# A convolution and SiLU block on one core: a new order of the steady block's steps

## The chip, the cores and the metric

The kernel runs on one core of one Trainium2 chip. The metric is the device time of one execution in microseconds (us). Three runs are shown for the kernel before, and the median counts. Engine names are those of the profile: PE multiplies, PEld loads weights for it, DVE is the vector engine, ACT the scalar engine, POOL is GpSimd, and SP issues transfers.

## The reference

The input x has 8 sequences of 4096 tokens with 192 channels, all float32. A causal depthwise convolution with 7 taps comes first; its taps are a softmax over 7 weights for each of 8 heads (24 channels each). Its result, 32768 tokens by 192, goes through a two-layer block without a bias:

```
out[s] = sum over k of softmax(weight)[head, k] * x_padded[s + k]     # 7 taps
h = out @ w_in        # 192 -> 2048
g = h * sigmoid(h)    # silu
y = g @ w_out         # 2048 -> 192
```

## The kernel before

**Blocks and stages.** The tokens are worked in 32 blocks of 1024 (TT = 1024, two halves of 512 columns). The products use fewer multiplications than the plain formula: sums of inputs and of weights are formed so that 15 products stand for 18 in each of five groups of the first layer. For PE a block has two stages. In the first (the P stage below) 75 products and a plain rest make h; in the second (the D stage) 192 matmuls in 48 slots make y. The two alternate for the whole kernel: the P stage of block b, then the D stage of block b.

**Two lanes.** A product of the P stage has 64 rows of weights and 512 columns, and it takes either the upper or the lower half of PE's rows. I call these halves lane 0 and lane 1; `e` in `product` (L616 to L637) picks the lane, and `ON_B` (L599) lists the products of lane 1. Products of the two lanes run at the same time. Each product is two rows of the trace, since a float32 matmul is two passes. In a D slot four matmuls of 128 x 32 weights run side by side in the four column groups.

**The order is written out by hand.** Every engine works its own instructions in the order of issue, and that order is a string of steps. `START` serves the first blocks, and `PLAN` is run once for each later block, from b = 3 on (end of the function). A step is a name and digits, and a sign in front says which block it belongs to: none is block b, `-` is b - 1, `=` is b - 2, `+` is b + 1. The function `step` (L863) calls the helper. The steps are these:

| step | engine | what it does | line of the profile |
|---|---|---|---|
| `Pr.g` | PE | product r of group g, in a chain's PSUM bank | L630 |
| `L.nk` | PE | plain products of the rest; `L.1k` is two halves, one on each lane | L647 |
| `uo.g` | ACT | copy of the running sum of chain 0 to an SBUF tile u | L679 |
| `Xo.g`, `ao.g`, `bo.g` | DVE | add or subtract u, chain 1 (X, a) and chain 2 (b) | L673 |
| `So.g`, `SL.i` | ACT | silu into the tile g | L691, L696 |
| `t.ji` | DVE | differences of g tiles for the second layer | L714 |
| `Di.je` | PE | slot i of the second layer for tile j, half e | L746 |
| `x`, `y`, `z` / `M` | ACT / DVE | copies and sums that finish y | L804 to L824 |
| `o.i`, `st.i` | DVE, SP | transpose of y and three stores | L834, L843 |
| `ld.k`, `i.k` | SP, DVE | four loads of x for the block after next in `+` form, and their transpose | L181, L465 |
| `ha.0` | POOL, SP | the 6 columns of the convolution's past | L486, L487 |
| `v.ki` | ACT, POOL | tap i of channels k of the next block: ACT multiplies into a tile u, and POOL issues a transfer that adds it to nat (tap 0 is ACT alone) | L496, L499, L500 |
| `sp.k`, `w.i` | SP, DVE | copies of nat into dup, and the differences win, which are the products' inputs | L521, L538, L541 |

**What ties the steps together.** In a group, chain 0 is the products 5, 2, 6, 1, 0, 14 in one bank, and after each of the first five a `u` copies the sum before the next product may write. Chain 1 is 3, 9, 7, 4, 8 in a second bank: `X2` reads it after 3, `X4` after 9, `a5` after 7, `a1` after 4, `a0` after 8. Chain 2 is 12, 10 in bank 4, read by `b1` and `b5`. `S3` reads chain 0's bank at its end, and the next group in that bank may start only then. The groups run in the order 0, 4, 1, 2, 3. The slots D0 to D5 write banks 7, 1, 3, 5, 6 and 4, which the P stage uses too, so the last readers of one stage hold the first writers of the other (`P5.4` writes bank 1, and waits for `M2`, the last reader of D1's sum). The tile u comes from a list of ten (`free`): `u` and `v` take from its front, and a tile goes back to its end at once after `v` and after its `X` or `a`. So a `u` can be handed a tile that a POOL transfer is still reading, and then ACT waits for that transfer:

```python
            z = free.pop(0)
            pin(nc.scalar.activation(z, src, AF.Copy, scale=tap))
            pin(nc.gpsimd.dma_start(out=dst, in_=z, accum_op=ALU.add))
            free.append(z)
```

The taps of one k all add to the same nat, so the transfers of `v.k1` to `v.k6` follow one another. The tiles t and osb share three buffers, so `t.10` waits until the stores of the y before it have left.

Of the kernel before, what the change touches and what calls it, by code (L numbers as in the profile page):

```python
# [17 lines left out]
def kernel(  # L18
# [60 lines left out]


    PLAN = (
        "+ld.1 P5.0 | -P8.3 -S1.4 -a0.2 -S4.3 | -D0.00 -t.01 -S0.2 | -D1.00 -S1.2 =o.2 v.00 "
        "| -D2.01 -t.03 -S5.1 =st.2 | -D2.00 -b5.3 | -D1.20 -sp.0 v.21 -S5.3 | -D4.01 u5.0 "
        "-t.02 -S1.3 | -D5.01 -sp.2 | -D4.00 -t.10 | -D0.20 -t.11 | -D3.01 | -D0.11 -t.12 | "
        "-D1.30 v.22 | -D3.00 +ld.2 -t.13 | -D2.11 -a0.3 | -D5.00 | -D2.10 -t.20 -S0.3 | "
        "-D3.11 v.11 | -D5.10 | -D4.11 -w.0 | -D0.30 v.12 | -D4.10 -t.21 | -D1.11 -t.23 | "
        "-D0.21 | -D0.01 v.23 -w.1 | -D3.10 -t.22 | -D5.21 | -D0.31 | -D5.11 | -D1.10 -t.30 "
        "| -D1.01 -t.31 | -D2.20 | -D2.21 v.13 | -D5.20 | -D4.21 v.01 v.14 | -D4.20 v.24 | "
        "-D1.21 -w.2 | -D3.20 -t.33 | -D2.30 v.02 | -D1.31 -t.32 | -D2.31 -y1.0 | -D5.30 "
        "v.03 | -D0.10 v.25 | -D3.21 -z1.0 v.15 -y0.0 | -D4.31 -y2.0 -w.3 | -D5.31 -M1.0 | "  # L90
        "-D3.30 -x2.1 v.26 -x2.0 | -D4.30 -x2.2 -M2.0 | -D3.31 -w.5 -x0.0 -M3.0 | L.02 | "
        "P2.0 -x2.3 -w.4 | P5.4 | P3.0 u4.0 -M6.0 | L.12 v.16 u5.4 | L.00 | P6.0 -x1.0 -M4.0 "
        "| L.10 u2.0 | P2.4 | L.01 X2.0 | L.11 v.04 u4.4 | P9.0 | P1.0 SL.0 -M5.0 SL.2 | "
        "P6.4 | P13.0 u0.0 X4.0 SL.1 | P5.1 | P3.4 -M7.0 S2.0 +i.2 u2.4 | P0.0 | P7.0 X2.4 | "
        "P11.0 | P12.0 u1.0 a5.0 -o.1 | P9.4 | P1.4 S4.0 b1.0 -st.1 u5.1 | P13.4 | P4.0 X4.4 "
        "u0.4 | P10.0 | P2.1 a1.0 +ld.0 v.05 | P7.4 | P0.4 u4.1 b5.0 | P14.0 | P8.0 u1.4 "
        "v.06 S5.0 | P11.4 | P14.4 a5.4 S3.0 a0.0 S2.4 | P6.1 | P12.4 S3.4 | P4.4 | P3.1 "
        "u2.1 b1.4 S4.4 | P5.2 | P10.4 X2.1 | P1.1 a1.4 u5.2 | P9.1 b5.4 | P2.2 u0.1 | P8.4 "
        "X4.1 | P5.3 u4.2 | P7.1 a0.4 | P0.1 +i.1 u5.3 sp.1 | P12.1 a5.1 | P6.2 u1.1 | P3.2 "
        "-o.0 | P4.1 u2.2 b1.1 | P13.1 | P2.3 a1.1 | P10.1 S2.1 | P1.2 u4.3 X2.2 | P8.1 | "  # L100
        "P11.1 -o.3 u0.2 | P13.2 S1.1 a0.1 | P6.3 S4.1 | P9.2 +i.0 | P0.2 b5.1 u2.3 +ha.0 | "
        "P3.3 S0.0 X4.2 | P1.3 S2.2 | P12.2 u1.2 | P11.2 X2.3 | P7.2 u0.3 b1.2 | P14.1 S4.2 "
        "| P9.3 a5.2 S0.4 | P0.3 -st.0 | P10.2 S1.0 X4.3 | P14.2 u1.3 | P7.3 b5.2 +v.20 "
        "-st.3 | P4.2 S0.1 | P12.3 a5.3 S3.1 | P14.3 +v.10 a1.2 | P13.3 | P4.3 S5.2 b1.3 | "
        "P8.2 S2.3 | P11.3 a1.3 S3.3 | P10.3 S5.4 t.00 S3.2"
    )
    START = (
        "=dp.28 =v.20 =v.10 =dp.44 =v.00 =dp.18 =dp.6 =dp.40 =dp.7 =dp.32 =dp.23 =dp.30 "
        "=dp.13 =dp.2 =dp.20 =dp.24 =dp.15 =dp.35 =dp.14 =dp.33 =dp.11 -ld.1 =dp.37 =dp.36 "
        "=dp.25 -ld.2 =dp.27 =dp.17 -ld.0 =dp.0 =v.11 =dp.34 =v.01 =dp.26 =v.12 =dp.29 =v.21 "  # L110
        "=v.13 =dp.45 =v.22 =dp.21 =v.02 =dp.42 =v.14 =v.03 =dp.39 =v.15 =dp.3 =v.04 =dp.38 "
        "=v.16 =dp.47 =v.23 =sp.1 =v.05 =dp.1 =v.24 =dp.22 -i.1 =dp.12 =v.25 =v.06 =dp.43 "
        "=v.26 =go.2 =sp.0 =dp.19 -i.0 =dp.46 -i.2 =dp.31 -ha.0 =dp.9 =sp.2 =dp.4 =dp.41 "
        "-v.10 -v.00 -v.11 =dp.8 -v.20 -v.01 =dp.5 -v.12 =dp.16 -v.02 =w.0 =dp.10 =w.1 =cp.0 "
        "-L.01 -P5.0 -v.03 =cp.1 -L.02 -P5.4 =w.2 -u5.0 -L.10 =w.3 -u5.4 -P2.0 -P3.0 -v.13 "
        "-P2.4 -u4.0 -v.04 -P6.0 -L.00 -u4.4 -L.12 -u2.0 -L.11 -SL.0 -X2.0 -P6.4 -SL.2 =w.4 "
        "=cp.2 -P9.0 -P1.0 -u2.4 =o.0 -P13.0 -P5.1 -v.14 -u0.0 -X4.0 -P3.4 -P1.4 -S2.0 =w.5 "
        "-SL.1 -P7.0 -P11.0 -u5.1 -X2.4 -u0.4 -P12.0 -P0.0 -a5.0 -v.21 -P13.4 -P0.4 -u1.0 "
        "=o.1 -P4.0 -P9.4 -u1.4 -v.15 -S4.0 -P2.1 -P14.4 -a1.0 -b1.0 -P14.0 -P8.0 -u4.1 -X4.4 "
        "-S3.4 -P6.1 -P10.0 -v.22 -S2.4 -a0.0 -P11.4 -P7.4 -u2.1 -b5.0 -S3.0 -P5.2 -P3.1 "  # L120
        "-S4.4 -a5.4 -P1.1 -P12.4 -u5.2 -X2.1 -P4.4 -u0.1 -P9.1 -b1.4 -P2.2 -a1.4 -P10.4 "
        "-X4.1 -P5.3 -u4.2 -P8.4 =o.2 -P6.2 -b5.4 -P13.1 -u5.3 =st.2 -a0.4 -P0.1 -P7.1 -u2.2 "
        "-v.23 -S2.1 ld.1 -P2.3 -P3.2 -a5.1 -u1.1 -S0.0 -P1.2 -P12.1 -X2.2 -S0.4 -P4.1 -u4.3 "
        "-P13.2 -b1.1 ld.2 -S1.4 -P6.3 -a1.1 -u0.2 -P10.1 -v.24 -P11.1 -u2.3 -P8.1 -b5.1 "
        "-P0.2 -S4.1 -P9.2 -v.05 -S2.2 -a0.1 -P12.2 -P1.3 -u1.2 -X4.2 -S0.1 -P3.3 -P14.1 "
        "-b1.2 -u0.3 -S5.4 -P7.2 -P11.2 -X2.3 -v.16 -P10.2 -P0.3 -S4.2 -a5.2 -sp.1 -P9.3 "
        "-P14.2 -u1.3 -b5.2 -S3.1 -P13.3 -P4.2 -X4.3 -S3.2 -S1.0 i.1 -P14.3 -P12.3 =st.0 "
        "-S1.1 -a1.2 -P11.3 -P7.3 -S5.0 -v.06 -S1.2 -t.00 -D0.00 =st.1 -S3.3 -S2.3 -D1.20 "
        "-b1.3 -S5.1 ld.0 -S4.3 -t.01 -D0.01 -S5.2 -D0.21 -t.02 -D1.11 -sp.0 -a5.3 -D1.10 "
        "-v.25 -t.03 -P8.2 P5.0 +ld.1 -P4.3 -P10.3 -D1.30 -b5.3 -v.26 -D1.00 -a0.2 -sp.2 "  # L130
        "-D4.01 -t.10 -S0.2 -D5.00 -D2.01 i.0 -D4.00 -t.11 -D2.00 i.2 -D5.01 ha.0 -t.13 "
        "-D0.11 -D3.00 -a1.3 +ld.2 -D3.01 -t.12 v.10 -D4.11 -w.0 v.00 +ld.0 -D5.10 v.11 v.20 "
        "-D5.11 -D2.10 u5.0 -t.20 -D0.20 -w.1 -D3.11 -t.21 -D4.10 -w.2 -D2.11 -t.23 -P8.3 "
        "P2.0 -D0.31 -a0.3 -t.22 -D3.10 -S0.3 -S1.3 -D4.21 v.21 -S5.3 u4.0 v.01 -D4.20 -t.30 "
        "-D3.20 -D5.21 -t.31 -D2.20 -D5.20 -D2.21 -D0.10 -t.32 -D2.30 v.02 -D1.01 -t.33 "
        "-D0.30 v.03 -D1.31 v.12 -D2.31 v.04 v.22 -D1.21 v.05 -D3.30 -y1.0 -w.3 -z1.0 -D5.30 "
        "v.13 -D5.31 -D3.31 -x2.0 -M1.0 -x2.1 -D4.31 -x2.2 v.14 -x2.3 -y2.0 -M2.0 -D3.21 "
        "-y0.0 v.06 -D4.30 -x0.0 -w.4 v.23 -x1.0 P3.0 P5.4 -M3.0 L.10 u5.4 -w.5 P6.0 L.02 "
        "-M4.0 L.11 u2.0 L.00 P2.4 X2.0 P1.0 L.01 -M5.0 u4.4 v.15 L.12 u0.0 P6.4 P9.0 SL.2 "
        "SL.0 P0.0 P13.0 X4.0 SL.1 u2.4 -M7.0 P3.4 P5.1 S2.0 +i.0 P7.0 P1.4 u5.1 X2.4 P12.0 "  # L140
        "P11.0 u0.4 a5.0 u1.0 v.24 P9.4 P2.1 S4.0 b1.0 P4.0 P13.4 u4.1 X4.4 P14.0 P10.0 a1.0 "
        "P0.4 P7.4 S3.0 b5.0 v.25 P11.4 P8.0 u1.4 a5.4 S2.4 P6.1 P12.4 a0.0 P14.4 P4.4 u2.1 "
        "b1.4 v.26 P5.3 P3.1 S3.4 a1.4 S4.4 P10.4 P1.1 X2.1 P5.2 P8.4 -M6.0 u0.1 b5.4 P9.1 "
        "P0.1 u5.2 -o.1 u5.3 P13.1 P2.2 X4.1 -st.1 u1.1 +i.2 P12.1 P2.3 u4.2 a0.4 S2.1 P7.1 "
        "P6.2 b1.1 u4.3 P3.2 a5.1 P6.3 u2.2 P10.1 S5.4 X2.2 P4.1 u2.3 S0.4 P9.2 b5.1 P1.2 "
        "S0.0 a1.1 P13.2 P11.1 S1.0 -o.0 u0.2 P8.1 v.16 P1.3 S2.2 S4.1 sp.1 P0.2 P12.2 a0.1 "
        "u0.3 X4.2 S5.0 P3.3 P14.1 u1.2 +i.1 P7.2 P11.2 X2.3 -st.0 b1.2 P9.3 P0.3 S4.2 a5.2 "
        "+ha.0 P10.2 u1.3 X4.3 P4.2 S0.1 P7.3 b5.2 P14.3 S1.1 a1.2 S3.1 P12.3 P14.2 S3.3 a5.3 "
        "P13.3 -o.3 P4.3 S3.2 b1.3 -st.3 +v.10 P8.2 +v.20 a1.3 P10.3 P11.3 S5.2 t.00 S2.3"
    )  # L150
    QUEUE = (0, 4, 1, 2, 3)
    CHAIN_BANKS = ((0, 1, 7, 1, 0), (2, 3, 2, 3, 2), (4, 4, 4, 4, 4))
# [41 lines left out]
    x0 = x.flatten_outer_dims()[TB - pad : TB, :].rearrange("t (k c) -> c k t", k=NK)  # L194
# [651 lines left out]
                )  # L846
            )

    plan = [slot.split() for slot in PLAN.split("|")]
    did, later = set(), []  # L850
    closing = f"S3.{QUEUE[-1]}"
    BACK = {"-": 1, "=": 2, "+": -1}
# [263 lines left out]
```

## Time and profile before

| what | value |
|---|---|
| median of three runs | 2364.05 us (2362.52 to 2364.63) |
| span of the profiled execution, first to last instruction | 2358.8 us |
| median less this span | 5.25 us |
| PE busy | 2350.1 us (100%), x17630 |
| PEld busy | 1053.1 us (45%) |
| DVE busy | 1784.5 us (76%) |
| ACT busy | 1488.6 us (63%) |
| POOL busy | 531.0 us (23%) |
| mean granted TensorE clock | 0.999 |
| one P stage, 974.30 to 1010.46 us | 36.16 us |
| the D stage after it, 1010.46 to 1046.67 us | 36.21 us |

The profile is of one execution. It gives that execution's span, and not its whole time; the runs' median stands 5.25 us above the span. PE counts as busy while any matmul is under way, so a lane that stands still beside a working one does not show in the busy share. To see that, one has to read the starts of the single rows: two passes in one lane are 0.429 us apart when nothing holds them.

### The profile page before, as it was taken

What the parts mean: (1) busy time and instruction counts of PE and PEld (TensorE: products, weight loads), DVE (VectorE), ACT (ScalarE), POOL (GpSimd) and SP (SyncE); (2) the same over time, 40 slices, a digit from 0 to 9 for tenths busy, and PEclk for the clock granted to TensorE, in tenths of its full rate; (3) what the DMA queues carried; (4) which work ended last, traced back from release to release, by engine and by line L of the source; (5) the groups of instructions that cost most, each with busy time, mean ns of one, the idle gap of its engine ahead of it and who ended that gap; (6) DMA issues with size and microseconds to landing.
All of it is one profiled execution on the core that took longest, in us unless ns stands there. A gap on an engine that the chain in (4) does not pass through costs nothing.

```text
span 2358.8 us, 45531 instructions
## 1 busy us (share of the span) xinstructions
PE 2350.1 (100%) x17630; PEld 1053.1 (45%) x17630; DVE 1784.5 (76%) x2373; ACT 1488.6 (63%) x2779; POOL 531.0 (23%) x672
## 2 busy tenths in 40 slices
PE   9999999999999999999999999999999999999998
PEld 4344444444444444444444454444444444444445
DVE  8898767787777787777877777767778777787676
ACT  5346766667656677566676666765667756667643
POOL 4911122211222112222112221122211222211200
PEclk9999999999999999999999999999999999999999
DMA  7234667656566655666556656556655566565511
GB/s 158 51 66 72 107 106 125 105 103 107 98 121 107 106 105 95 119 116 106 106 106 109 119 99 109 105 99 122 107 106 101 101 116 116 106 109 98 96 23 25
DMA packets 523833, 238.81 MB, mean 101 GB/s; under 512 B 431648, under 2 KB 436768, under 8 KB 523616
## 3 DMA queue, kind: packets, MB, share of 16 engines
q0 software_dynamic: 73024, 133.73, 33.7%
q1 hardware_dynamic: 447392, 101.78, 23.1%
q8 instruction: 138, 2.26, 0.4%
q10 hardware_dynamic: 3200, 0.39, 0.1%
q14 instruction: 79, 0.65, 0.1%
HBM read 31.46 MB, written 25.17 MB: 24 GB/s over the span
## 4 chain that ended last, share of the span: by engine, by line
PE 98%; DVE 1%; DMA 0%; ACT 0%; SPq 0%; issue 0%; ACTq 0%
PE ps L746 47%; PE ps L630 42%; PE ps L647 5%; PE ps L767 2%; PE ps L576 2%; PE ps L1015 1%; DVE t L714 0%; DMA dup<-nat 0%; PE ps L423 0%; ACT g L691 0%; DMA nat<-u 0%; SPq L843 0%; DVE g L673 0%; DVE cmb L163 0%; ACT u L163 0%
## 5 line engine op out<-in xcount | busy, mean ns | idle before, releaser
L500 POOL DMA_DIRECT2D nat<-u x504 | 431.9, 957 | 1598.0 <-ACT u L499 643.4
L630 PE MATMUL ps<-win,wr 64*128 64x512 f32 x1550 | 721.5, 598 | 0.0
L746 PE MATMUL ps<-g,wo 128*32 128x512 f32 x2976 | 703.0, 593 | 0.0
L630 PE MATMUL ps<-win,ws 64*128 64x512 f32 x1550 | 638.3, 599 | 0.9 <-ACT u L679 0.9
L746 PE MATMUL ps<-t,wo 128*32 128x512 f32 (+2 forms) x4528 | 547.8, 446 | 0.0
L679 ACT COPY u<-ps 128x512 f32<-128x512 f32 x775 | 442.5, 587 | 136.7 <-PE ps L630 88.6
L746 PE MATMUL ps<-t,wx 128*32 128x512 f32 x2976 | 495.6, 592 | 0.6 <-DVE t L714 0.5
L630 PE MATMUL ps<-dup,wr 64*128 64x512 f32 x868 | 424.1, 597 | 0.0
L691 ACT ACTIVATE g<-g 128x512 f32<-128x512 f32 x465 | 286.2, 633 | 175.5 <-DVE g L673 175.5
L714 DVE TENSOR_TENSOR t<-g,t 128x1024 f32<-128x1024 f32 x248 | 302.0, 1218 | 109.7 <-PE ps L746 107.4
L714 DVE TENSOR_TENSOR t<-g 128x1024 f32<-128x1024 f32 x248 | 302.5, 1220 | 103.9 <-PE ps L746 82.7
L809 ACT COPY yx<-ps 32x512 f32<-32x512 f32 x150 | 86.8, 579 | 421.5 <-PE ps L746 419.4
L673 DVE TENSOR_TENSOR g<-u,ps 128x512 f32<-128x512 f32 x465 | 314.2, 681 | 42.8 <-PE ps L630 32.0
L499 ACT ACTIVATE u<-xt,taps 128x512 f32<-128x512 f32 x504 | 340.0, 717 | 1.1
L630 PEld LDWEIGHTS ps<-win,wr 64*128 64x128 f32 x1550 | 272.1, 186 | 139.5 <-issue 75.6
L630 PE MATMUL ps<-dup,ws 64*128 64x512 f32 x682 | 328.2, 598 | 0.0
L630 PEld LDWEIGHTS ps<-win,ws 64*128 64x128 f32 x1550 | 255.8, 186 | 135.3 <-issue 58.6
L746 PEld LDWEIGHTS ps<-t,wo 128*32 128x32 f32 x4528 | 188.5, 110 | 273.3 <-issue 266.0
L691 ACT ACTIVATE g<-ps 128x512 f32<-128x512 f32 x465 | 267.8, 599 | 36.2 <-PE ps L630 33.6
L673 DVE TENSOR_TENSOR ps<-u,ps 128x512 f32<-128x512 f32 x310 | 215.0, 694 | 64.3 <-PE ps L630 26.7
L746 PE MATMUL ps<-g,wx 128*32 128x512 f32 x1488 | 250.5, 592 | 0.0
L824 DVE TENSOR_TENSOR cmb<-cmb,ps 96x512 f32<-96x512 f32 x150 | 102.2, 681 | 181.7 <-ACT yx L809 180.7
(92 smaller groups left out, 2010.5 us busy)
## 6 DMA issues: line engine op xcount, KB each, us to landing
nat<-u POOLq DMA_DIRECT2D x504, 256.0 KB, 4.0
dup<-nat SPq DMA_DIRECT2D x345, 128.0 KB, 3.0
nat<-in_x_dram SPq DMA_DIRECT2D x382, 64.0 KB, 2.7
out_dram<-osb SPq DMA_DIRECT2D x376, 64.0 KB, 2.0
raw<-in_moe_w_out_dram SPq DMA_DIRECT2D x8, 384.0 KB, 3.5
raw<-in_moe_w_in_dram SPq DMA_DIRECT2D x12, 192.0 KB, 4.4
ws<-wr POOLq DMA_DIRECT2D x8, 192.0 KB, 5.0
raw<-in_moe_w_in_dram SPq DMA_DIRECT2D x6, 128.0 KB, 3.0
```

What stands on the lines that cost most here:

```text
L499: pin(nc.scalar.activation(z, src, AF.Copy, scale=tap))
L500: pin(nc.gpsimd.dma_start(out=dst, in_=z, accum_op=ALU.add))
L576: nc.tensor.matmul(hs[a, n, e], rows(wr[j], e)[:, a, k, :], rows(d, e)[:, n, k, :], start=k == 0, stop=k == NK - 1,)
L630: nc.tensor.matmul(to[:, cols], raw(g, *LEFT[e][r], e), rhs[:, cols], start=first, stop=True, skip_group_check=True,)
L647: nc.tensor.matmul(banks[PLAIN_BANKS[n and 1 + e]][:, cols], rows(wr[j] if own == e else ws[j], e)[:, a, k, :], rows(dups[b], e)[:, SLOT[e ...
L673: pin(nc.vector.tensor_tensor(out_, u, v, op=op))
L679: pin(nc.scalar.copy(us[b, g, o][:, cols], t1[:, cols]))
L691: pin(nc.scalar.activation(h, src, AF.Silu))
L714: pin(nc.vector.tensor_tensor(t[i // 2][:, i % 2, :], u, v, op=ALU.subtract))
L746: nc.tensor.matmul(accs[b][at][SQ * q : SQ * q + SQ, to], lhs[:, e, SQ * k : SQ * k + SQ], rhs[:, e, ts(q, TB // 4) if i == 5 else to], st ...
L809: pin(nc.scalar.copy(to, acc[3 * (name[0] == "x") + k][n:P, :]))
L824: pin(nc.vector.tensor_tensor(out_, u, v, op=ALU.add))
```

## The change

`PLAN` gets another order. The bars between slots go, and with them nothing else, since the loop ran through all slots in a row before as well. The multiset of a cycle's steps is the same, but some steps at the seam of two cycles are now counted in the neighbouring one: `=o.2 =st.2` become `-o.2 -st.2`, `-S1.4` becomes `S1.4`, `v.21` becomes `+v.21`, `+v.10` becomes `v.10`, and `S0.1`, `S1.1`, `S2.3`, `S5.4`, `a1.3`, `P10.3` and `t.00` move behind the seam with a `-`. `START` keeps its order and gets four steps at its end, so that the seam fits (its other lines in the diff are only broken anew). No step's operation, tile or bank changes.

```diff
     PLAN = (
-        "+ld.1 P5.0 | -P8.3 -S1.4 -a0.2 -S4.3 | -D0.00 -t.01 -S0.2 | -D1.00 -S1.2 =o.2 v.00 "
-        "| -D2.01 -t.03 -S5.1 =st.2 | -D2.00 -b5.3 | -D1.20 -sp.0 v.21 -S5.3 | -D4.01 u5.0 "
-        "-t.02 -S1.3 | -D5.01 -sp.2 | -D4.00 -t.10 | -D0.20 -t.11 | -D3.01 | -D0.11 -t.12 | "
-        "-D1.30 v.22 | -D3.00 +ld.2 -t.13 | -D2.11 -a0.3 | -D5.00 | -D2.10 -t.20 -S0.3 | "
-        "-D3.11 v.11 | -D5.10 | -D4.11 -w.0 | -D0.30 v.12 | -D4.10 -t.21 | -D1.11 -t.23 | "
-        "-D0.21 | -D0.01 v.23 -w.1 | -D3.10 -t.22 | -D5.21 | -D0.31 | -D5.11 | -D1.10 -t.30 "
-        "| -D1.01 -t.31 | -D2.20 | -D2.21 v.13 | -D5.20 | -D4.21 v.01 v.14 | -D4.20 v.24 | "
-        "-D1.21 -w.2 | -D3.20 -t.33 | -D2.30 v.02 | -D1.31 -t.32 | -D2.31 -y1.0 | -D5.30 "
-        "v.03 | -D0.10 v.25 | -D3.21 -z1.0 v.15 -y0.0 | -D4.31 -y2.0 -w.3 | -D5.31 -M1.0 | "
-        "-D3.30 -x2.1 v.26 -x2.0 | -D4.30 -x2.2 -M2.0 | -D3.31 -w.5 -x0.0 -M3.0 | L.02 | "
-        "P2.0 -x2.3 -w.4 | P5.4 | P3.0 u4.0 -M6.0 | L.12 v.16 u5.4 | L.00 | P6.0 -x1.0 -M4.0 "
-        "| L.10 u2.0 | P2.4 | L.01 X2.0 | L.11 v.04 u4.4 | P9.0 | P1.0 SL.0 -M5.0 SL.2 | "
-        "P6.4 | P13.0 u0.0 X4.0 SL.1 | P5.1 | P3.4 -M7.0 S2.0 +i.2 u2.4 | P0.0 | P7.0 X2.4 | "
-        "P11.0 | P12.0 u1.0 a5.0 -o.1 | P9.4 | P1.4 S4.0 b1.0 -st.1 u5.1 | P13.4 | P4.0 X4.4 "
-        "u0.4 | P10.0 | P2.1 a1.0 +ld.0 v.05 | P7.4 | P0.4 u4.1 b5.0 | P14.0 | P8.0 u1.4 "
-        "v.06 S5.0 | P11.4 | P14.4 a5.4 S3.0 a0.0 S2.4 | P6.1 | P12.4 S3.4 | P4.4 | P3.1 "
-        "u2.1 b1.4 S4.4 | P5.2 | P10.4 X2.1 | P1.1 a1.4 u5.2 | P9.1 b5.4 | P2.2 u0.1 | P8.4 "
-        "X4.1 | P5.3 u4.2 | P7.1 a0.4 | P0.1 +i.1 u5.3 sp.1 | P12.1 a5.1 | P6.2 u1.1 | P3.2 "
-        "-o.0 | P4.1 u2.2 b1.1 | P13.1 | P2.3 a1.1 | P10.1 S2.1 | P1.2 u4.3 X2.2 | P8.1 | "
-        "P11.1 -o.3 u0.2 | P13.2 S1.1 a0.1 | P6.3 S4.1 | P9.2 +i.0 | P0.2 b5.1 u2.3 +ha.0 | "
-        "P3.3 S0.0 X4.2 | P1.3 S2.2 | P12.2 u1.2 | P11.2 X2.3 | P7.2 u0.3 b1.2 | P14.1 S4.2 "
-        "| P9.3 a5.2 S0.4 | P0.3 -st.0 | P10.2 S1.0 X4.3 | P14.2 u1.3 | P7.3 b5.2 +v.20 "
-        "-st.3 | P4.2 S0.1 | P12.3 a5.3 S3.1 | P14.3 +v.10 a1.2 | P13.3 | P4.3 S5.2 b1.3 | "
-        "P8.2 S2.3 | P11.3 a1.3 S3.3 | P10.3 S5.4 t.00 S3.2"
+        "-sp.0 P5.0 v.22 -S1.2 -S4.3 -P10.3 -sp.2 -a1.3 -S5.4 -P8.3 -D0.21 -D1.11 -D1.00 -S0.1 "
+        "-t.00 -t.01 -a0.2 -D2.01 -t.03 v.23 -D4.01 -S0.2 -D4.00 -S1.1 -D2.00 -S5.1 v.00 -t.10 "
+        "-b5.3 -D0.11 -D5.00 -t.11 -D1.01 -D2.11 v.10 v.11 -t.13 -D4.10 -a0.3 -D5.11 -D5.01 "
+        "-D0.00 -S2.3 -t.02 -D0.20 -D5.10 -t.12 u5.0 -D3.11 -D3.00 -D3.01 v.01 v.02 -D4.11 "
+        "-D2.10 -D0.31 -D3.10 -D1.21 -t.20 -t.21 -D2.21 -D2.20 -t.22 -t.23 -D4.20 -D4.21 -D5.20 "
+        "-S5.3 -D1.10 -D0.01 -S0.3 v.12 -S1.3 -t.30 v.13 -D0.10 v.03 v.04 -D0.30 v.14 -D3.21 "
+        "-y0.0 -z1.0 -w.0 -w.1 -t.31 -t.33 -D5.31 -w.2 -t.32 -w.3 v.24 v.25 v.15 -D2.30 v.05 "
+        "v.26 -D5.21 +ld.2 -w.4 -D1.30 -D5.30 -D4.31 -D1.20 -D2.31 -D4.30 v.06 -x2.0 -x2.1 +i.2 "
+        "-D1.31 -y1.0 -D3.31 -x2.3 -D3.20 -D3.30 L.02 -y2.0 -w.5 P2.0 L.01 +ld.0 +i.0 v.16 "
+        "-M1.0 -M6.0 -x2.2 -x1.0 u4.0 -M2.0 P5.4 u5.4 L.10 P6.0 P3.0 -M3.0 -M4.0 -o.1 -x0.0 "
+        "u2.0 X2.0 P2.4 u4.4 L.11 L.12 SL.1 SL.2 L.00 P9.0 SL.0 P1.0 u0.0 P6.4 u2.4 P13.0 S2.0 "
+        "-M5.0 P3.4 -o.3 P5.1 P0.0 X4.0 u1.0 -M7.0 P7.0 P12.0 P1.4 P11.0 X2.4 P9.4 u5.1 u0.4 "
+        "a5.0 P4.0 P13.4 P0.4 b1.0 P10.0 P2.1 P14.0 S4.0 X4.4 P7.4 a1.0 P8.0 S2.4 b5.0 P12.4 "
+        "-o.0 u1.4 P14.4 u4.1 P11.4 S1.0 S4.4 a5.4 P6.1 a0.0 b1.4 P3.1 P4.4 P10.4 -o.2 S3.4 "
+        "P5.2 u2.1 P1.1 X2.1 a1.4 b5.4 P9.1 X4.1 P8.4 S3.0 P5.3 u5.2 P2.2 P7.1 a0.4 u0.1 P0.1 "
+        "S0.0 -st.2 S5.0 a5.1 u4.2 u5.3 P12.1 u1.1 b1.1 S0.4 -st.0 P6.2 u2.2 P13.1 P4.1 a1.1 "
+        "P3.2 S2.1 X2.2 P2.3 u4.3 P10.1 b5.1 P1.2 u0.2 P8.1 +ld.1 P11.1 P9.2 S4.1 P6.3 -st.3 "
+        "u2.3 P13.2 a0.1 P0.2 P3.3 P1.3 S2.2 +i.1 P12.2 sp.1 u1.2 u0.3 X4.2 P7.2 P11.2 P14.2 "
+        "X2.3 S1.4 P9.3 b1.2 P0.3 a5.2 P10.2 S4.2 X4.3 P4.2 b5.2 P7.3 a1.2 S3.2 P14.1 P12.3 "
+        "u1.3 P14.3 S5.2 P13.3 S3.1 a5.3 P4.3 S3.3 +ha.0 +v.20 -st.1 +v.21 P11.3 P8.2 b1.3"
     )
     START = (
...
-        "P13.3 -o.3 P4.3 S3.2 b1.3 -st.3 +v.10 P8.2 +v.20 a1.3 P10.3 P11.3 S5.2 t.00 S2.3"
+        "P8.2 +v.20 a1.3 P10.3 P11.3 S5.2 t.00 S2.3 -o.2 -st.2 S1.4 +v.21"
     )
 ...
-    plan = [slot.split() for slot in PLAN.split("|")]
+    plan = [PLAN.split()]
```

## The prediction

> **What bounds the kernel now.** I read the page first, then the chain of waits, the waits, and the timelines of single places.
>
> ```profile
> span 2358.8 us, 45531 instructions
> PE 2350.1 (100%) x17630; PEld 1053.1 (45%) x17630; DVE 1784.5 (76%) x2373; ACT 1488.6 (63%) x2779; POOL 531.0 (23%) x672
> ```
>
> PE is never idle for long, so a time can only come from how densely its two lanes are filled. The chain of waits, cut to one block, gives the period:
>
> ```profile
> 938.15 36.23 PE ps L746 x384
> ...
> 979.30 31.22 PE ps L630 x139
> 1010.53 36.22 PE ps L746 x384
> ```
>
> From one D stage to the next are 72.38 us. The rows in a D stage stand 0.429 us apart: 8 x (5 x 0.858 + 0.219) = 36.07 of its 36.22 us, so nothing is to be had there. The P stage has 72.37 - 36.22 = 36.15 us in most blocks. In it each lane has 40.5 slots of two passes (36 products on lane 0, 39 on lane 1, and 4.5 or 1.5 plain ones), 40.5 x 0.858 = 34.75 us. So 1.40 us a block are lost, 0.09 of them to the change of stage. The rest is steps that wait in both lanes. One place, in the block that begins at 974.30, shows the form (PE, then its weight loads, then DVE):
>
> ```profile
> 992.67 0.59 PE L630 MATMUL ps<-win,ws 64*128 64x512 f32 x1
> 993.10 0.59 PE L630 MATMUL ps<-win,ws 64*128 64x512 f32 x1
> 993.69 0.69 PE L630 MATMUL ps<-win,wr 64*128 64x512 f32 x1
> ```
> ```profile
> 993.69 0.18 PEld L630 LDWEIGHTS ps<-win,wr 64*128 64x128 f32 x1 [0.24 <-DVE ps L673]
> ```
> ```profile
> 992.94 0.70 DVE L673 TENSOR_TENSOR ps<-u,ps 128x512 f32<-128x512 f32 x1
> ```
>
> The first two are the passes of P8.4, and P7.1 could start at 993.53. It starts at 993.69, 0.05 after X4.1 has left its bank, and its weight load is not hidden, which costs 0.105 more (its second pass comes 0.534 later, not 0.429). Read in this way, lane 0 loses 0.105 at L.02 (the first load after the D stage), 0.171 at P9.0, 0.125 at P14.4, 0.258 at P10.4, 0.118 at P9.1, 0.266 at P7.1 and 0.266 at P7.3: 1.31 us, and 34.75 + 1.31 + 0.09 = 36.15. Lane 1 loses less.
>
> Some blocks are longer. Of the 28 P stages between 248.5 and 2280 us 19 take 36.15 or 36.16 us and nine take 36.32 to 37.13; the excess is 4.0 us together, and one D stage has 1.0 more: 5.1 us. This is what such a block shows (ACT, POOL, PE in the P stage that begins at 1554.76):
>
> ```profile
> 1576.01 1.56 ACT L679 COPY u<-ps 128x512 f32<-128x512 f32 x3 [2.44 <-DMA nat<-u]
> ```
> ```profile
> 1572.69 0.85 POOL L500 DMA_DIRECT2D nat<-u  x1 [4.91 <-DMA dup<-nat]
> ```
> ```profile
> 1576.65 0.69 PE L630 MATMUL ps<-win,ws 64*128 64x512 f32 x1 [0.52 <-ACT u L679]
> ```
>
> ACT's u4.2 was handed the tile that the POOL transfer of v.06 still read. In the waits this is "ACT u L679 <- DMA nat<-u", 28.3 us in 24 blocks. In a quiet block u4.2 starts 19.6 us after the P stage begins, 0.08 after the landing, and P6.2 behind it has nothing to spare; each lateness of v.06 is paid in full.
>
> **The change part by part.** No instruction is added or removed, so each part is an order. I follow each queue with the durations of the rows (u 0.585, silu 0.595 to 0.633, X 0.695, other sums 0.683 to 0.689, neighbours on ACT overlapping by 0.105 and on DVE by 0.085) and the hand-offs of the rows: a product's reader starts 0.589 + 0.037 after its second pass began, 0.07 more if it waits for two semaphores; a weight load follows 0.054 after the reader's end.
>
> *Same-lane neighbours.* The old PLAN alternates lanes in pairs (01, 10). The new one has runs such as P7.4 P8.0 P12.4 P14.4 (lane 0) ahead of P11.4 P6.1 (lane 1). If lane 1 may start behind a product of lane 0 that is still waiting for its lane, this costs nothing. START has such a place, "P9.2 ... P12.2 P1.3" with P12.2 on lane 0, and P1.3 on lane 1:
>
> ```profile
> 128.97 1.55 PE L630 MATMUL ps<-win,ws 64*128 64x512 f32 x5
> 130.02 1.02 PE L630 MATMUL ps<-win,wr 64*128 64x512 f32 x2
> ```
>
> P12.2 is the wr at 130.02; the five ws rows before it are one of P0.2, two of P9.2 and both of P1.3. P1.3 began at 129.40, 0.63 ahead of P12.2, although it stands behind it in the order. I take zero. The other end: with starts strictly in order, filling the lanes by the new order takes 44 slots instead of 40.5, 3.5 x 0.858 = 3.0 us a block, or 2.2 if P9.1's and P7.1's waits (0.51 and 0.27, below) fall into the same pauses. The Trainium skill, page "TensorE: Matmul & The Clock Gate", Part 3, "The mechanism", says that matmuls start and end in program order, a strict FIFO; by it the sum would be that other end. The two rows above disagree, by 0.63 us.
>
> *Waits in lane 0.* P14.4 moves behind P12.4. Its own wait for u1.4 goes (-0.125), and P10.4's wait for b1.4 (-0.258), since P12.4 is now a slot earlier. But X2.1, on which P9.1 waits, hangs on S3.4 and u2.1 behind P14.4: 0.429 + 0.589 + 0.037 + 0.595 - 0.105 + 0.585 + 0.033 + 0.07 + 0.695 + 0.054 + 0.105 = 3.09 us from P14.4's start to P9.1's, and only three slots (2.57) lie between, where four were. P9.1 loses 0.51 instead of 0.118. P7.1 and P7.3 still stand two slots behind P9.1 and P9.3, with X4 between: 0.19 to 0.266 each, as before. P9.0 keeps about its 0.17 to 0.20, L.02 its 0.105. Sum 1.27 to 1.35 against 1.31.
>
> *Waits in lane 1.* P5.4 is now second behind P2.0 and waits for bank 1, through y1, y2, M1, M6, M2 behind D1.31, which is fourth from the D stage's end instead of tenth. D1.31 begins 3.43 before the stage's end; 1.02 + 0.037 + 0.579 + 0.025 + 0.256 + 0.025 + 0.579 (x2.3 stands between) + 0.1 + 0.683 + 0.604 + 0.598 + 0.054 + 0.105 = 4.67 us brings P5.4 0.2 behind its slot. With 0.1 at P1.0, P5.2, P6.2, P1.3 each and 0.16 at P5.3 lane 1 loses some 0.9, less than lane 0, so this decides nothing up to about 0.4 us more. I take -0.02 us a block for both lanes (-0.6 in 28 blocks), with bounds of 0.1 either way (2.8 us), the scatter of my chains against the old rows.
>
> *The taps.* A transfer of POOL lands after 4.0 us (median), and the next tap of the same k is issued 0.53 later. In the old order v.04, v.05 and v.06 sit in the P stage and v.06 is issued 16.3 us into it. In the new one ACT has all taps done by the first P slots, and the chain v.24, v.25, v.26, v.06, v.16 ends 7 to 8 us into the stage. The first copies that are handed these tiles are u5.1 and u0.4, 2.6 to 2.9 us after the landings. So the 28.3 us of waits and the 4.0 us of excess go, as long as the chain is less than 2.6 us late; in the old trace v.06 was up to 1.6 late. In the long D stage it was t.10 that stood, for the buffer that the stores st.2 were leaving:
>
> ```profile
> 1381.47 1.23 DVE L714 TENSOR_TENSOR t<-g 128x1024 f32<-128x1024 f32 x1 [3.57 <-DMA dup<-nat]
> ```
>
> The view names another transfer of SP's queue, which came just before; the stores had been issued from 1375 us on. In the new order the last store is issued some 10 us ahead of t.10. I take -4.6 of the 5.1 us (bounds 0 and -5.1).
>
> *SP and DVE.* SP's queue now runs st.2, st.0, ld.1, st.3, sp.1, ha.0, st.1 in a row behind o.2 at 0.555 us an issue. ld.1's last issue is then 5.0 us behind o.2, and lands 2.4 to 3.3 later; i.1 on DVE needs it, 9.4 us behind o.2. Margin 1.1 to 2, cost nothing. ha.0 lands 5 us ahead of v.20. In the D stage t.03 ends 0.7 ahead of D4.01 and t.13 0.8 ahead of D4.10, where t.01 had 0.1 ahead of D2.01: nothing.
>
> *The ends.* START's order stays. The last P stage ends on more waits: +0.2.
>
> Sum: -0.6 - 4.6 + 0.2 = -5.0; span 2353.8, and with the 5.25 between span and median 2359.0 us. The three runs lie within 2.1 us, and about 0.2% (4.7 us) is what a measurement can tell from no change; the sum is at this bound.
>
> **The rivals.** *The excess stays in part* (0.18): the chain of taps is late elsewhere (its first links now meet SP's sp and ld transfers), and u5.1 or u0.4 pay; half is gained, 2361.7. For it speaks v.21, which landed 5.7 us after its issue beside sp transfers; against it, the 2.6 us. *Lane 0 loses less* (0.14): P9.1's chain is shorter by 0.15 us a block since lane 1 has room, 2354.8. *DVE held by i.1* (0.08), slower: an issue of SP took up to 2.3 us at times. From 2 us of delay behind o.2 on, i.1 holds X4.2 and with it P11.2 and P7.2; 1 us in each block gives 28 us less the margin's share, 2375 to 2387. *Starts in order* (0.04): 28 x 2.2 to 3.0, 2421 to 2443. *The forecast* (0.56): 2359.0, by its bounds 2355 to 2362.
>
> **How the numbers follow.** The forecast's -5.0 lies just beyond 4.7, so 0.30 of its 0.56 count as faster, and with the second rival that makes 0.44. The other 0.26 and the first rival make 0.44 within 0.2%, and the two slow rivals 0.12. The range 2354 to 2367 takes in the first three cases and small delays of i.1; it leaves out what lies beyond.
>
> **What would show it.** Right: a P stage of 36.1 to 36.2 us in nearly every block, no copy that waits for a nat transfer for long, a gap near 0.4 at P9.1 and none at P10.4, and rows of lane 1 ahead of earlier ones of lane 0. Wrong: P stages of 38 us (starts in order), DVE waiting for in_x transfers, or ACT waiting for nat<-u at u5.1.

## The result and the profile after

The changed kernel takes 2398.71 us (median of 4 runs, 2394.81 to 2403.85) against 2364.34 us of the kernel before in the same session (4 runs, 2362.52 to 2365.74). The ratio is 1.0148, with a 95% interval of 1.0133 to 1.0163: slower, where 2359.0 and at most 2367 were forecast. The profiled execution's span went from 2358.8 to 2395.3 us, +36.5. The head of its page:

```profile
span 2395.3 us, 45524 instructions
PE 2374.3 (99%) x17630; PEld 1125.2 (47%) x17630; DVE 1794.3 (75%) x2373; ACT 1510.0 (63%) x2779; POOL 532.8 (22%) x672
```

Every engine works as many instructions as before, and PE is still never idle for long. The loss shows when PE's rows are cut into stages. All 29 D stages from 212 us on take 36.22 us; the one long D stage of before is gone. Of the 29 P stages ten take 36.71 us, 0.56 more than the 36.15 of most blocks before; I call these ten quiet. Nineteen take 36.77 to 41.36, together 25.3 us above 36.71. So there are two losses: 29 x 0.56 = 16.2 us in every block, and 25.3 us in some. Less the excess of before, 4.0 us of P stages and 1.0 of a D stage, they make the 36.5 us; what the last P stage and the two ends add and save, 0.2 to 0.4 us each, nearly cancels.

**The loss in some blocks.** The chain of waits in the block whose P stage begins at 1949.2 us (start, duration, what):

```profile
1942.73 6.06 DMA nat<-u
1949.07 1.07 POOL nat L495 x2
1950.14 5.20 DMA nat<-u
1955.38 0.47 issue
1955.87 0.52 POOL nat L495
1956.40 4.28 DMA nat<-u
1960.77 0.59 ACT u L674
1961.40 26.08 PE ps L625 x110
1987.48 36.22 PE ps L741 x384
```

The chain no longer runs on PE alone. The transfer of v.24 takes 6.06 us, that of v.05 5.20, that of v.16 4.28, and when it has landed, ACT may make its copy u0.4, and PE goes on. The timeline of ACT and PE in another such block (P stage from 1065.81 us) shows the two copies:

```profile
1075.75 0.59 ACT L674 COPY u<-ps 128x512 f32<-128x512 f32 x1 [0.66 <-DMA nat<-u]
1077.30 0.58 ACT L674 COPY u<-ps 128x512 f32<-128x512 f32 x1 [0.97 <-DMA nat<-u]
```
```profile
1077.94 0.69 PE L625 MATMUL ps<-win,wr 64*128 64x512 f32 x1 [0.79 <-ACT u L674]
```

u5.1 waits 0.66 us for the transfer of v.06, u0.4 another 0.97 for that of v.16. Both were handed the tile which that transfer still read. P0.4 and P10.0 behind them then leave both lanes empty for 0.79 us. The waits (engine, what waits, for what: us in total, times, longest us):

```profile
ACT u L674 <- DMA nat<-u: 31.1, 31, 2.4
```

Before, the same wait had 28.3 us, at u4.2. It was forecast to vanish, and it has moved to u5.1 and u0.4 (in the first P stage, of 41.36 us, u4.4 and u2.4 wait as well).

**The loss in every block.** A quiet block, P stage from 917.68 us, PE and then ACT:

```profile
931.43 0.59 PE L625 MATMUL ps<-win,ws 64*128 64x512 f32 x1
931.44 0.69 PE L625 MATMUL ps<-dup,wr 64*128 64x512 f32 x1
931.86 0.59 PE L625 MATMUL ps<-win,ws 64*128 64x512 f32 x1
931.97 0.59 PE L625 MATMUL ps<-dup,wr 64*128 64x512 f32 x1
932.29 0.59 PE L625 MATMUL ps<-dup,ws 64*128 64x512 f32 x1
932.40 0.59 PE L625 MATMUL ps<-win,ws 64*128 64x512 f32 x1
932.72 0.59 PE L625 MATMUL ps<-dup,ws 64*128 64x512 f32 x1
```
```profile
933.36 1.08 ACT L686 ACTIVATE g<-ps 128x512 f32<-128x512 f32 x2 [1.59 <-PE ps L625]
934.33 0.59 ACT L674 COPY u<-ps 128x512 f32<-128x512 f32 x1
```

`win,ws` at 931.43 and 931.86 is P12.4, `dup,wr` at 931.44 and 931.97 is P11.4, `dup,ws` at 932.29 and 932.72 is P14.4 (lane 0); `win,ws` at 932.40 is P6.1. The order is P12.4, P14.4, P11.4. P11.4's lane had been free for 0.22 us, but P11.4 starts with P12.4's first pass. And S4.4, which reads P11.4's bank, starts at 933.36: 1.39 us after P11.4's second pass began, but 0.64 after P14.4's, the usual distance of a reader. ACT stood idle for 1.59 us. S3.4, P14.4's own reader, is the second of the two rows, behind S4.4; u2.1 follows at 934.33, then X2.1, then P9.1, whose lane has waited 0.845 us (0.95 with the 0.105 that its weight load costs when nothing hides it). Read in this way, lane 0 loses 0.105 at L.02, 0.336 at L.00, 0.950 at P9.1, 0.197 at P7.1, 0.266 at P7.3: 1.85 us, and 34.75 + 1.85 + 0.09 = 36.69.

### The profile page after: what moved, and what is told of

The parts are those of the page before. It is cut to its first block, busy times and chain, and to the rows that moved or that the text cites. A ratio compares the mean times of both kernels' runs of the same rounds, so it can differ in the third digit from the quotient of the medians.

```text
span 2395.3 us, 45524 instructions
## 1 busy us (share of the span) xinstructions
PE 2374.3 (99%) x17630; PEld 1125.2 (47%) x17630; DVE 1794.3 (75%) x2373; ACT 1510.0 (63%) x2779; POOL 532.8 (22%) x672
## 5 line engine op out<-in xcount | busy, mean ns | idle before, releaser
L741 PE MATMUL ps<-g,wo 128*32 128x512 f32 x2976 | 695.3, 593 | 0.0
L625 PE MATMUL ps<-win,wr 64*128 64x512 f32 x1550 | 673.8, 597 | 13.8 <-ACT u L674 13.5
L625 PE MATMUL ps<-win,ws 64*128 64x512 f32 x1550 | 667.2, 596 | 0.0
L741 PE MATMUL ps<-t,wo 128*32 128x512 f32 (+2 forms) x4528 | 538.9, 446 | 0.0
L741 PE MATMUL ps<-t,wx 128*32 128x512 f32 x2976 | 464.4, 592 | 0.0
L625 PE MATMUL ps<-dup,wr 64*128 64x512 f32 x868 | 439.0, 602 | 0.0
L625 PEld LDWEIGHTS ps<-win,wr 64*128 64x128 f32 x1550 | 264.4, 186 | 165.0 <-issue 64.5
L625 PE MATMUL ps<-dup,ws 64*128 64x512 f32 x682 | 340.2, 592 | 0.0
L686 ACT ACTIVATE g<-g 128x512 f32<-128x512 f32 x465 | 278.3, 626 | 46.8 <-DVE g L668 46.8
L741 PEld LDWEIGHTS ps<-t,wx 128*32 128x32 f32 x2976 | 122.0, 110 | 257.7 <-issue 246.7
```

The source lines that it names most:

```text
L625: nc.tensor.matmul(to[:, cols], raw(g, *LEFT[e][r], e), rhs[:, cols], start=first, stop=True, skip_group_check=True,)
L686: pin(nc.scalar.activation(h, src, AF.Silu))
L741: nc.tensor.matmul(accs[b][at][SQ * q : SQ * q + SQ, to], lhs[:, e, SQ * k : SQ * k + SQ], rhs[:, e, ts(q, TB // 4) if i == 5 else to], st ...
```

## The experiments

Two theories were tried. **A** has two parts. (1) A product pass starts only when at most three passes ahead of it in the order have not started, and its end is told to its reader only when those ahead of it have ended, so that a run of one lane holds the readers of the other. (2) The tiles of v.06 and v.16 come free too late. **B** says that those waits are the data's own, and that the late taps hurt in other ways. The steps here are those of `PLAN`; ratios are to the kernel before, run beside each.

**e1_tiles: the choice of the tile.**

```diff
-                us[b, g, o] = free.pop(0)
+                k = next((k for k, z in enumerate(free) if id(z) not in tapped), 0)
+                us[b, g, o] = free.pop(k)
+                tapped.discard(id(us[b, g, o]))
...
             free.append(z)
+            tapped.add(id(z))
```

> The changed kernel, except that a copy u takes the first free tile whose last reader was a sum on DVE, and only without one the tile of a tap. Theory A (the P stages over 36.71 us, 25.3 us together, are copies u5.1 and u0.4 that were handed the tiles which the transfers of v.06 and v.16 still read): all P stages 36.7 us, no copy of ACT waits for nat<-u, span 2395.3 - 25.3 = 2370 (2368 to 2373). Rival B (the taps are simply done too late, and what needs nat or the queues behind them pays as well): P stages still of 37 to 39 us with another wait, span 2385 or more.

2371.63 us, ratio 1.0029 (1.0018 to 1.0041), span 2369.7. All P stages are 36.70 or 36.71 us but one of 36.95, and no copy u waits for a transfer. In the waits of ACT the place is taken by a small one that no lane feels:

```profile
ACT u L677 <- DVE ps L669: 22.1, 27, 0.8
```

So the 25.3 us are the tiles that still fed a transfer, those of u5.1 and u0.4 above all; the spread of the runs falls with them, from 9 us to 0.7.

**e2_lanes: the two places with a run of one lane.**

```diff
-        "... P2.4 u4.4 L.11 L.12 SL.1 SL.2 L.00 P9.0 ..."
+        "... P2.4 u4.4 L.00 L.11 L.12 SL.1 SL.2 P9.0 ..."
-        "... P12.4 -o.0 u1.4 P14.4 u4.1 P11.4 S1.0 S4.4 ..."
+        "... P12.4 -o.0 u1.4 P11.4 P14.4 u4.1 S1.0 S4.4 ..."
```

> The changed kernel with two products moved: L.00 ahead of L.11, and P11.4 ahead of P14.4, so that no product of one lane stands behind more than one product of the other lane that is still waiting. Theory A (a pass starts only when at most three passes ahead of it in the order have not started, and the end of a product is told to its reader only when those ahead of it have ended): L.00 loses nothing (0.336 us less), S4.4 and then S3.4 are 0.4 to 0.5 us earlier and P9.1 loses 0.5 instead of 0.95 us; the shortest P stage is 36.0 to 36.2 instead of 36.71 us. The copies u5.1 and u0.4 come earlier and wait up to 0.4 us more, so span 2378 to 2388. Rival B (these waits are the data's own: L.00's bank, S4.4's sum): L.00 starts again 4.20 us into the stage, P9.1 has its gap of 0.85, shortest P stage 36.6 to 36.7, span 2393 to 2397.

2388.37 us, ratio 1.0099 (1.0081 to 1.0116), span 2387.9. The shortest P stage is 36.20 us, as A has it. The excess over it grew to 33.1 us: v.16 now lands 11.0 us into the stage (median), not 10.6.

**e3_both.** The edits of e1_tiles and e2_lanes together.

> Both edits in the changed kernel, the choice of the tile and the two products moved. If the two causes are the whole loss: P stages 36.0 to 36.2 us throughout, span 2395.3 - 25.3 - 28 x 0.6 = 2353 (2350 to 2357), some 0.2 to 0.4% under the kernel before. If something else of the new order costs time: span 2362 or more.

2356.89 us, ratio 0.9968 (0.9955 to 0.9980), span 2355.0; 28 P stages of 36.20 us and one of 36.44. The new order without its two faults is 0.3% faster than the old one. Lane 0 loses 0.105 at L.02, 0.179 at P9.0, 0.163 at P7.4, 0.443 at P9.1, 0.197 at P7.1 and 0.266 at P7.3, 1.35 us.

**e10_p11_alone.** The second line of e2_lanes' edit alone, with e1_tiles' tiles.

> The kernel of e1_tiles with P11.4 ahead of P14.4 alone; L.00 stays behind L.12. By the sum of waits in lane 0: L.00 keeps its 0.336 us and P9.0 none; P9.1 loses 0.44 to 0.5 instead of 0.95; P stage 36.71 - 0.34 to 0.5 = 36.2 to 36.4. If the two places do not add up (the later start of everything behind L.00 covers P9.1's wait): 36.6 to 36.7.

2357.04 us (one run), span 2355.3, P stage 36.20 us. L.00 keeps its 0.336 us, and P9.0 and P7.4, which had 0.342 in e3_both, lose nothing. So moving L.00 is worth nothing, and the whole 0.51 us a block of e3_both against e1_tiles belongs to P11.4.

**e7_silu_order.** In e1_tiles, S3.4 ahead of S4.4 on ACT.

```diff
-        "... P11.4 S1.0 S4.4 a5.4 ... -o.2 S3.4 P5.2 u2.1 ..."
+        "... P11.4 S1.0 S3.4 S4.4 a5.4 ... -o.2 P5.2 u2.1 ..."
```

> The kernel of e1_tiles with one step of ACT moved: S3.4 ahead of S4.4; PE's order is the changed kernel's. Theory A (S4.4 is told of P11.4's end only when P14.4, ahead of it in the order, has ended, and S3.4 stood behind S4.4 on ACT): S3.4 starts 0.63 us after P14.4's second pass has begun, 0.5 earlier than now, P9.1 loses 0.45 to 0.5 instead of 0.95 us, P stage 36.2 to 36.3 instead of 36.71. Rival B (what counts is that P11.4 itself starts late): P9.1 keeps 0.8 to 0.95, P stage 36.6 to 36.7.

2371.65 us (one run), P stage 36.69 us: the gain that A expected did not come. S3.4 did start 0.63 us after P14.4's second pass, but S4.4 still stood ahead of u2.1, on which P9.1 hangs. The edit was the wrong one for the question; the next puts it right.

**e7b_silu_order.** In e1_tiles, S4.4 behind u2.1.

```diff
-        "... P11.4 S1.0 S4.4 a5.4 ... S3.4 P5.2 u2.1 ..."
+        "... P11.4 S1.0 a5.4 ... S3.4 P5.2 u2.1 S4.4 ..."
```

> The kernel of e1_tiles with one step of ACT moved: S4.4 behind u2.1, so that neither S3.4 nor u2.1 stands behind it; PE's order is the changed kernel's. Theory A (S4.4, whose data P11.4 had given earlier, was told so only at P14.4's end, and S3.4 and u2.1 stood behind it): u2.1 starts 0.5 us earlier against P14.4, P9.1 loses 0.44 to 0.5 instead of 0.95 us, P stage 36.2 to 36.3 instead of 36.71. Rival B (P11.4's late start itself is what counts): P9.1 keeps 0.8 to 0.95, P stage 36.6 to 36.7.

2359.34 us (one run), span 2357.6, P stage 36.27 us, P9.1 loses 0.442. The timeline of PE and ACT, P stage from 901.58 us, shows P14.4's second pass and then S3.4, u2.1, and S4.4 with S3.0:

```profile
916.62 0.59 PE L626 MATMUL ps<-dup,ws 64*128 64x512 f32 x1
```
```profile
917.25 0.60 ACT L689 ACTIVATE g<-ps 128x512 f32<-128x512 f32 x1 [1.57 <-PE ps L626]
917.74 0.58 ACT L677 COPY u<-ps 128x512 f32<-128x512 f32 x1
918.21 1.10 ACT L689 ACTIVATE g<-ps 128x512 f32<-128x512 f32 x2
```

u2.1 now stands 1.12 us behind the pass instead of 1.61. PE's order is as in the changed kernel, P11.4 starts as late as there, and P9.1 has lost its extra wait: it was S4.4 in ACT's line, and B is out.

**e6_run_of_four: the rule by itself.** In e3_both, a run of four ready products of lane 0 ahead of one of lane 1.

```diff
-        "... P10.1 b5.1 P1.2 u0.2 P8.1 +ld.1 P11.1 P9.2 S4.1 P6.3 ... P13.2 a0.1 P0.2 P3.3 ..."
+        "... P10.1 b5.1 P8.1 P9.2 P13.2 P1.2 u0.2 +ld.1 P11.1 S4.1 P6.3 ... a0.1 P3.3 P0.2 ..."
```

> The kernel of e3_both with P8.1, P9.2 and P13.2 moved ahead of P1.2: eight passes of lane 0 (P10.1, P8.1, P9.2, P13.2) stand ahead of P1.2 of lane 1, and none of them waits for data. Theory A (a pass starts only when at most three ahead of it have not started, and its end is told in order): P1.2's first pass starts together with P9.2's first, 1.7 us after P10.1's first and 1.2 us after its lane came free, and its reader u0.2 starts 0.63 us after P13.2's second pass has begun and not 0.63 after P1.2's own. The lane that waits is lane 1: P stage 36.8 to 37.2 us. Strict order of starts: P1.2 starts with or after P13.2's second pass, 3.0 us after P10.1's first; P stage 38. Free lanes: P1.2 starts 0.5 us after P10.1's first as before, P stage 36.2.

2390.66 us (one run), span 2389.0, P stage 37.35 us in nearly every block. The timeline of PE and of ACT, P stage from 911.0 us:

```profile
933.97 0.59 PE L626 MATMUL ps<-dup,ws 64*128 64x512 f32 x1
...
934.40 0.59 PE L626 MATMUL ps<-dup,ws 64*128 64x512 f32 x1
934.83 1.02 PE L626 MATMUL ps<-win,wr 64*128 64x512 f32 x2
935.69 1.13 PE L626 MATMUL ps<-win,ws 64*128 64x512 f32 x4
936.55 1.13 PE L626 MATMUL ps<-dup,wr 64*128 64x512 f32 x4
```
```profile
937.64 0.59 ACT L677 COPY u<-ps 128x512 f32<-128x512 f32 x1 [2.41 <-PE ps L626]
```

P10.1 begins at 933.97. The row of four at 935.69 is P9.2 and P1.2: P1.2's first pass starts 0.01 after P9.2's, with three passes ahead of it unstarted (P9.2's second and P13.2's two). Lane 1 had been empty for 1.242 us. P1.2's second pass begins at 936.23, P13.2's at 936.98, and u0.2, which reads P1.2's bank, starts at 937.64: 0.66 after the latter, 1.41 after its own. Both halves of the rule hold. The block pays 1.15 us, a little more than the 0.6 to 1.0 expected: P1.3 waits for u2.3, behind u0.2 on ACT, and P12.2 of the other lane, behind P1.3 in the order, waits 1.005 us with it, though its own lane is free from 938.26 on and its bank's last reader, b5.1, ended at 935.71.

**e5_taps: the chains side by side.** The tile choice is the changed kernel's own.

```diff
-        "... v.01 v.02 ... v.12 ... v.03 v.04 ... -w.3 v.24 v.25 v.15 -D2.30 v.05 v.26 ..."
+        "... v.01 v.24 v.02 ... v.12 v.25 ... v.03 v.26 v.04 ... -w.3 v.15 -D2.30 v.05 ..."
```

> The changed kernel with three taps earlier, so that the three chains of taps run side by side: v.24 behind v.01, v.25 behind v.12, v.26 behind v.03; the choice of tiles is the changed kernel's own. Theory A (a transfer takes 3.3 us alone, 4.3 as the second and 5.2 as the third in POOL's line, and the next of the same k comes 0.5 after the landing): v.16 lands 6 to 7 us into the P stage instead of 10.6, u5.1 and u0.4 wait for nothing, all P stages 36.71 us, span 2370 (2368 to 2374). Rival B (taps that come earlier on ACT delay the silus, or meet the sp transfers): D stages over 36.22, or copies that still wait for nat<-u; span 2380 or more.

2374.37 us, ratio 1.0039 (1.0027 to 1.0052), span 2371.7. v.16 lands 7.6 us into the P stage (median; 9.3 at the latest, the first P stage aside), where 6 to 7 was expected, and outside the first P stage no copy u waits (two do there, 2.4 us). The taps wait instead, where nothing hangs on it:

```profile
ACT u L494 <- DMA nat<-u: 63.1, 58, 2.5
```

28 P stages are 36.70 to 36.72, the first after `START` 38.91, all D stages 36.22. So the late transfers came from the taps' own order.

**e4_before_tiles.** The choice of the tile in the kernel before.

> The kernel before with the choice of the tile alone. Theory A: the nine P stages over 36.15 us lose their excess (4.0 us), the one long D stage stays, span 2358.8 - 4.0 = 2354.8, time ratio 0.998. Rival (the long stages of before have another cause): span 2358 to 2360, ratio 1.000.

2363.69 us, ratio 0.9996 (0.9987 to 1.0004): no gain. The wait for nat<-u is gone, and the P stages' excess falls from 4.0 to 1.4 us, but now every P stage takes 36.25 instead of 36.15, and five D stages take 4.1 us more than 36.22 (one took 1.0 before). The waits of this kernel tell why (ACT, and DVE):

```profile
ACT u L682 <- DVE ps L674: 48.6, 112, 1.0
```
```profile
DVE t L717 <- DMA out_dram<-osb: 12.9, 21, 3.6
DVE t L717 <- DMA dup<-nat: 11.4, 4, 3.8
```

A tile taken straight after the sum that freed it makes the copy wait for that sum, 112 times instead of once (0.3 us) before, and 28 x 0.1 = 2.8 us eat up the 2.6 us by which the P stages' excess fell. In each of the five long D stages t.10 waits 3.3 to 3.8 us, under both names in the last two lines. Whether the D stages differ from execution to execution or through this edit is open. The part of the expectation on the P stages' excess held, the one on the time did not.

**e8_better.** In e3_both, one more slot of lane 0 ahead of P9.1.

```diff
-        "... u2.1 P1.1 X2.1 a1.4 b5.4 P9.1 X4.1 P8.4 S3.0 P5.3 u5.2 P2.2 P7.1 ... P12.1 u1.1 ..."
+        "... u2.1 a1.4 P1.1 P8.4 X2.1 b5.4 P9.1 X4.1 S3.0 P5.3 u5.2 P12.1 P2.2 P7.1 ... u1.1 ..."
```

> The kernel of e3_both with P8.4 ahead of P9.1, P12.1 ahead of P7.1 and a1.4 ahead of X2.1 on DVE, so that four slots of lane 0 instead of three lie between P14.4 and P9.1. By the sum of waits in lane 0: P9.1's 0.44 us fall to 0.12 or less, P7.1 keeps 0.2 to 0.3; P stage 36.20 to 35.75 to 35.95, span 2355 - 28 x 0.35 = 2345 (2341 to 2350). Rival: P8.4 now waits for a1.4, or lane 1 (0.78 us of waits against 1.36) becomes the bound; P stage 36.1 to 36.3, span 2353 to 2358.

2361.24 us, ratio 0.9983 (0.9974 to 0.9992), span 2359.5, P stage 36.33: worse than e3_both. P9.1's 0.443 are gone, but P8.4 loses 0.204 (it waits for a1.4, which starts 0.64 us after the second pass of P3.1, ahead of P4.4 in the order, and not after that of P4.4, which a1.4 reads), P3.2 0.193 and P8.1 0.182.

**e9_better.** In e3_both, P14.4 first.

```diff
-        "... P8.0 S2.4 b5.0 P12.4 -o.0 u1.4 P11.4 P14.4 u4.1 S1.0 S4.4 ... b1.4 P3.1 P4.4 P10.4 -o.2 S3.4 ..."
+        "... P8.0 S2.4 b5.0 u1.4 P14.4 P11.4 P12.4 -o.0 u4.1 S1.0 S3.4 S4.4 ... -o.2 b1.4 P3.1 P4.4 P10.4 ..."
```

> The kernel of e3_both with P14.4 ahead of P11.4 and P12.4, and on ACT S3.4 ahead of S4.4, on DVE o.2 ahead of b1.4. By the sum of waits in lane 0: S3.4 comes 0.86 us earlier, so P9.1 loses nothing instead of 0.44, and P10.4 waits for b1.4, which waits for P12.4: 0.2 to 0.26. P stage 36.20 - 0.2 = 36.0 (35.95 to 36.1), span 2349 (2347 to 2352). Rival: u1.4, now ahead of more of PE's steps, holds P14.4 and both lanes behind it: P stage 36.2 or more.

2354.66 us, ratio 0.9956 (0.9942 to 0.9969), span 2352.9: faster than both kernels. P9.1 loses nothing, P10.4 0.258, P7.1 0.236; P stage 36.09, close to the 36.0 expected, and the span 0.9 us above the range expected.

## Why the prediction was wrong, point by point

**"Same-lane neighbours: I take zero."** This step failed. It was read from one row, P1.3 of `START`, which starts 0.63 us ahead of P12.2 and has only three passes to overtake, both of P12.2 and the second of P9.2; from that I concluded that any number can be overtaken. Counted over all 5208 rows of the P stages' products and plain products in the profile before (starts within 0.013 us taken as one moment), some 3960 starts have nothing unstarted ahead of them, some 1235 one pass, 9 two and 1 three; that one is P1.3. The old order never asked for more, so it could not show the limit. After the change 355 have two, 133 three, none four. What it cost, however, was not the starts: P11.4's late start and L.00's 0.336 us are covered, to within 0.07 us a block (e7b, e10). It was the end told late, through S4.4, S3.4 and u2.1, which stand in one line on ACT: 0.51 us a block, 29 x 0.51 = 14.8 us. The other 0.05 of the 0.56 us are lane 0's sum of waits in e3_both, 1.35 us, against 1.31 before. The other end of the bound, 2.2 to 3.0 us a block for starts strictly in order, was too far: the truth was a window of four passes. The Trainium skill, page "TensorE: Matmul & The Clock Gate", Part 3, "The mechanism", says that matmuls start and end in program order. For the ends the runs agree, as far as readers are told of them (u0.2 0.66 us behind P13.2's second pass, not behind P1.2's); for the starts they do not (up to three passes overtaken).

**"P9.1 loses 0.51."** It lost 0.950. The chain P14.4, S3.4, u2.1, X2.1, P9.1 was right: without S4.4 in it P9.1 loses 0.44 (e3, e7b, e10). The missing term was S4.4, which I had run before P14.4's end, when P11.4's own data was there. The gains forecast at P14.4 and P10.4 came (0.125 and 0.258). With P11.4 ahead of P14.4 the block's sum in lane 0 is 1.35 us against the 1.27 to 1.35 forecast, and the P stage 36.20 against 36.13. That the sum fits is partly luck: the 0.163 at P7.4 was not in the forecast, and P9.1's term was 0.07 too high.

**"The taps: -4.6 of 5.1 us."** This step failed too, and in its sign: the 5.1 us of before went, but 25.3 us came in their place, some +20 instead of -4.6. The mis-sized term is the transfer: I put 4.0 us, the median of all, on every link. The times from issue to landing go by the place in POOL's line (medians of the profile after, us):

| place among transfers issued back to back | transfers | issue to landing |
|---|---|---|
| first | v.02, v.13, v.25, v.06 | 3.3 |
| second | v.12, v.03, v.15, v.16 | 4.3 |
| third | v.24, v.05 | 5.2 |

v.04 has 3.4; two lie between the rows (v.26 with 4.0, v.14 with 4.7). The five taps at the head of the chain, v.21, v.22, v.23, v.11 and v.01, take 0.4 to 1.2 us more than their places would give (3.7 to 5.8); SP's transfers to dup and of x run beside them, and whether those are the reason was not tested. The run e5_taps bears the places out: there v.15 is first instead of second and lands after 3.3 us, and v.05 is second instead of third and lands after 4.3. The new order puts v.24 third behind v.04 and v.14, v.25 behind it, and v.05 third again, with v.06 behind that. So, the first P stage aside, v.06 lands 9.0 us into the stage (11.0 at the latest) and v.16 10.6 (12.3) instead of 7 to 8. The same order also moved the copies forward: free of waits, u5.1 starts at 9.17 us and u0.4 at 9.70, where the old order had 9.99 and 10.45. With 4.0 us for each link from the issue of v.24 on the sum comes to about 7, so the term, and not the chain, was at fault. The rival "the excess stays in part" named the place and kept half the gain; it did not think of a loss there. The reading "each lateness of v.06 is paid in full" was too strict as well. Before, the P stage keeps its 36.15 us until u4.2 starts 20.26 us after the stage begins (the block at 1119.05), some 0.6 later than the 19.6 of a block without lateness, and only what lies beyond is paid. Two of the nine long stages (248.53 and 1845.24) have u4.2 at 19.7 and 19.8, and so another cause, which stays open.

**"In the D stage t.10 stood."** Right: the last store is now issued 11.0 us ahead of t.10 (median), where some 10 were forecast, instead of 2.3. All D stages are 36.22 us, and no t waits for out_dram<-osb; before, the waits had

```profile
DVE t L714 <- DMA out_dram<-osb: 10.4, 22, 1.5
```

**SP and DVE.** Right: DVE waits 0.6 us in all for in_x, once. **Lane 1** decided nothing: in e3_both it loses 0.78 us. **The ends**: the last P stage took 36.71 us and not 35.87, +0.8 for the +0.2 forecast.

**Open.** Why every third P stage of the changed kernel from 474 us on is quiet, while the two between do not stay so, was not settled. In the quiet ones v.24 lands 4.7 to 5.4 us after its issue and v.05 after 5.2 to 5.3; in the stage after a quiet one it is v.05 that takes longer (5.6 to 6.7), in the next one v.24 (5.1 to 6.3). The tiles t and osb change among three buffers too, but no run ties the two together.

## What to carry to other kernels

The two lanes of PE ran apart here, but only by three passes, and their readers were told of ends in the order in which the products were issued. So interleave the lanes in issue order, and do not put a reader of the late lane ahead of the critical one on its own engine: one such reader cost 0.51 us a block here, with both lanes' slots unchanged.

For a chain of transfers take the time by the place in the queue (here 3.3, 4.3, 5.2 us), not the median, and ask what is handed the buffer that the last of them reads. And where a rule is read from one row, look for the row in which it would have failed: if the old order never tries it, the cost is bounded, not known.

## What the runs showed of the hardware

- A product pass starts ahead of at most three passes that stand before it and have not started: 5208 rows in each of the thirteen profiles, none with four. A run of eight passes of one lane held a ready pass of the other 1.242 us (e6).
- The end of a pass reaches its reader in the order of issue: 1.39 and 1.41 us after its second pass began, instead of the usual 0.63, each time 0.64 to 0.66 behind the pass ahead of it (S4.4 in the changed kernel, u0.2 in e6). In the changed kernel 296 of the 2325 readers have a pass ahead of their product in the order that began after the product's own second pass, and none of them starts less than 0.64 us behind it.
- A pass that waits for data holds the other lane too: P12.2 stood 1.005 us behind P1.3 (e6).
- Transfers of 256 KB that are issued back to back on POOL's queue land 3.3, 4.3 and 5.2 us after their issue in the changed kernel (medians), about 0.95 us more for each place; those that run beside SP's transfers to dup and of x take 0.4 to 1.2 us longer.
